# The factor that ScalarE copies out of PSUM: inverse sums in place of the values' products

## The chip, the cores and the metric

The kernel runs on one core of a Trainium2 chip. The metric is the device time of one execution in microseconds (us); less is better. Three runs of the kernel before took 791.66, 791.16 and 791.1 us, so the median is 791.16 us. The engines of the core are named as the profile names them: PE is TensorE's matmul, PEld its weight load, DVE VectorE, ACT ScalarE, POOL GpSimd, SP the queue that issues all DMAs.

## The reference

Eight batches of block-causal attention with eight heads each feed a gated feed-forward block. The two parts in short:

```python
scores = scale * np.matmul(q, k.transpose(0, 1, 3, 2))     # q, k, v: 8 x 8 x 576 x 64
scores = np.where(block_i >= block_j, scores, -1e9)        # blocks of 64 positions
attn = np.exp(scores - np.max(scores, axis=-1, keepdims=True))
attn = attn / (np.sum(attn, axis=-1, keepdims=True) + 1e-09)
out = np.matmul(attn, v)                                   # -> x: 8 x 576 x 512
...
h = gelu(x @ w_in)                                         # 512 -> 1024
u, v = h[..., :512], h[..., 512:]
v_n = (v - mu) / np.sqrt(var + 1e-06) * g_ln
gated = u * (np.einsum('ts,bsd->btd', w_sg, v_n) + b_sg[None, :, None])
y = x + gated @ w_out
```

The change touches only the division by the sums: the kernel multiplies the values' products by the inverse sums, after the product with `v`.

## The kernel before

**Pairs and slots.** The 64 heads are worked in 32 pairs of two; a pair has one *slot* (`slot`, L743), and four slots make a batch. Slot n turns (transposes) the probabilities of pair n and multiplies them with the values, while the scores of pair n+1 are computed in steps in between. Into the slot up to seven *holes* are put (`hole`), each one accumulation of the feed-forward block of an earlier batch. Slots 0 to 3 have no such work to put in: the feed-forward block of batch 0 is queued only when slot 3 is written.

**Order.** PE's order is the order of the code (its instructions are pinned, `kept`); that of ACT, DVE, POOL and SP is made by a scheduler that knows the dependencies. So an edit of the program's code moves other instructions on these engines.

**PSUM.** There are eight banks of 512 numbers per partition. Five (`sbank`) hold score products (tiles `s`), the values' products `ob` and the accumulations of the holes (`accv`, `accu`, `accs`, `acco`). Three (`pbank`) hold transposed data: `pa`, `pb`, `pc` (transposed probabilities, two tiles each per slot), `pd` (of `turn_first`) and `pe` (the transposed inverse sums). With three banks and eight such tiles a slot, the first turns of a slot wait for the last tiles of the slot before to be read out.

**What a slot does, in order.** `inverse` (L443): DVE adds and inverts the row sums (`ri`), POOL spreads them over 64 columns for each head (`rx`). `turn0` writes `pa` twice; ACT copies one into SBUF (`pt`), DVE the other. `turn2` does the same with `pb`. Then come the scores of the next pair: PE writes products into `s`, DVE takes the masked maxima (operation CUSTOM_DVE, `prob<-s`) and ACT the exponents. `av0` starts the values' products in `ob`, `turn1` writes `pc`, two further score steps follow, `turn_first` writes the first 64 positions' probabilities to `pd`. `turn_sums` (L461) transposes the inverse sums of the first 64 positions into columns 128 to 255 of `pd` and those of the other 512 into `pe`. `av1` ends `ob` and `av00` (L488) writes the product of the first 64 positions into columns 256 to 319 of `pd`.

**The end of the slot.** `normalise` (L492) takes a page `x` of 576 columns (one of three buffers shared with the reloaded pages `xr`), lets ACT copy `ob` and the first positions' product into it, lets DVE multiply it in place by `pe` and by the part of `pd`, and issues the store `spill<-x`. `split` (L502) then makes `xh` on DVE (a cast) and, from it, the low parts on POOL; the feed-forward block of that batch multiplies these. `split_qk` prepares the pair after the next: a cast `qk_h` on DVE and two subtractions `qk_l` on POOL.

**Names of the steps.** Below, "pa1" is the second `pa` of a slot, "pb" its first `pb` turn, "the boundary 1 to 2" the stretch in which slot 1 ends and slot 2 begins.

Of the kernel before, what the change touches and what calls it, by code (L numbers as in the profile page):

```python
# [9 lines left out]
F32 = mybir.dt.float32  # L10
# [4 lines left out]
ALU = mybir.AluOpType  # L15
# [13 lines left out]
def kernel(  # L29
# [13 lines left out]
    B, H, D, S = qT.shape  # L43
    P = 128
    BLK = 64
# [23 lines left out]
    def page(dtype, n, name):  # L69
        tag, bufs = KINDS.get(name, KINDS["w"])  # L70
        return sp.tile([P, n], dtype, tag=tag, name=name, bufs=bufs)

    def bank(tag, name, bufs):
        return psum.tile([P, 512], F32, tag=tag, name=name, bufs=bufs)

    def sbank(name):
        return bank("s", name, 5)

    def pbank(name):
        return bank("p", name, 3)  # L80
# [3 lines left out]
    def pin(ins, e):  # L84
        return tc.keep_in_program_order(ins) if e in kept else ins
# [4 lines left out]
    def turn(out, in_, identity):  # L90
        return pin(nc.tensor.transpose(out, in_, identity), "P")  # L91
# [11 lines left out]
    V, A, G, SP = Pinned(nc.vector, "V"), Pinned(nc.scalar, "A"), Pinned(nc.gpsimd, "G"), Pinned(nc.sync, "S")  # L103

    def copy(e, dst, src):
        return {"v": V.tensor_copy, "a": A.copy, "g": G.tensor_copy}[e](dst, src)
# [46 lines left out]
    t = sbank("warm")  # L153
# [15 lines left out]
    for s in (0, 1):  # L169
        t = cp.tile([P, NT, 2 * D], F32, name=f"v_f{s}")  # L170
# [5 lines left out]
    for s in range(4):  # L176
        row = []
        for i in range(NT):
            t = cp.tile([P, P * (i + 1) if i else BLK], F32, name=f"prob{s}_{i}")
# [209 lines left out]
    class Values:  # L389
# [71 lines left out]
        def turn_sums(self):  # L461

            turn(self.t4[:, 128:256], self.rx[:, 0, :], ident)
            t = self.rp = pbank("pe")
            for i in range(1, NT):
                turn(t[:, (i - 1) * P : i * P], self.rx[:, i, :], ident)

        def av(self, dst, j, pts, c0, n, start, stop):
            for a in (0, 1):
                r = slice(a * D, (a + 1) * D)  # L470
                mm(dst[r, :], self.v[:, j, r], pts[a][:, c0 : c0 + n], start=start, stop=stop)
# [19 lines left out]

        def normalise(self):  # L492

            x = self.x = page(F32, S, "x")
            copy("a", x[:, BLK:], self.ob)
            copy("a", x[:, :BLK], self.o0)
            V.tensor_tensor(x[:, BLK:], self.rp, x[:, BLK:], op=ALU.mult)
            V.tensor_tensor(x[:, :BLK], self.t4[:, 128:192], x[:, :BLK], op=ALU.mult)
            spill[self.b, self.p] = dp.tile([P, S], F32, tag="spill", name="spill", bufs=12)
            SP.dma_start(spill[self.b, self.p], x)  # L500

# [380 lines left out]
```

## Time and profile before

| | before |
|---|---|
| median of three runs | 791.16 us |
| the profiled execution | 792.08 us |
| its span, first to last instruction | 790.2 us |
| mean granted TensorE clock | 0.978 |
| ACT COPY x<-ob, 128x512, 32 times | 586 ns each |
| ACT COPY x<-pd, 128x64, 32 times | 217 ns each |
| DVE TENSOR_TENSOR x<-pe, 128x512, 32 times | 686 ns each |
| DVE TENSOR_TENSOR x<-pd, 128x64, 32 times | 213 ns each |

All four operations read PSUM and write the page x. A row of the timeline gives the start, the duration, the engine, the line, the operation with its tiles (written, then read), and in brackets the time that the engine sat idle before it and what ended that. A helper records every operation, so most rows have L88, L91 or L101; the tiles tell which step it is.

### The profile page before, as it was taken

To read this page: it belongs to the slowest core of one execution; us is meant where nothing else is said; L and a number is where in the kernel's file an instruction comes from. 1 tells how busy PE (TensorE), PEld (TensorE's weight loads), DVE (VectorE), ACT (ScalarE), POOL (GpSimd) and SP (SyncE) were. 2 spreads that over 40 slices of the span, in tenths; PEclk is the share of its full clock that TensorE was granted. 3 is DMA by queue.
4 is the path that set the end of the run, shared out by engine and by line. 5 is a ranking of instruction groups with operands and counts; after the bars stand their busy time and mean duration, and the time that the engine had idled before them with its cause. 6 is when DMAs were issued, how large, how long until landed. Compare 5 with 4: busy or idle time off the path is not lost. (4 is left out here: it accounts for less than half of the span.)

```text
span 790.2 us, 15821 instructions
## 1 busy us (share of the span) xinstructions
PE 761.1 (96%) x5926; PEld 639.9 (81%) x5926; DVE 499.7 (63%) x1457; ACT 450.0 (57%) x1172; POOL 267.9 (34%) x331
## 2 busy tenths in 40 slices
PE   7777998999999999999999999999999999999998
PEld 5554786877888888887888888888888978888998
DVE  5897578885757466563866648565676647633532
ACT  4775689567844478435974368544793358721600
POOL 4354255552424113351133414231233510322121
PEclk9897799999999999999999999999999999999999
DMA  7143224212241024311042122410233101320042
GB/s 239 61 126 118 89 91 141 88 61 75 78 149 60 2 76 122 106 61 52 25 136 90 61 76 62 145 50 32 77 106 121 61 19 59 105 76 31 1 121 75
DMA packets 46911, 65.66 MB, mean 83 GB/s; under 512 B 4082, under 2 KB 22514, under 8 KB 46836
## 3 DMA queue, kind: packets, MB, share of 16 engines
q1 hardware_dynamic: 46836, 64.67, 25.6%
q8 instruction: 46, 0.75, 0.4%
q14 instruction: 29, 0.24, 0.1%
HBM read 45.78 MB, written 18.87 MB: 82 GB/s over the span
## 5 line engine op out<-in xcount | busy, mean ns | idle before, releaser
L101 ACT ACTIVATE prob<-prob,negm 128x448 f32<-128x448 f32 (+4 forms) x320 | 176.4, 554 | 40.6 <-DVE negm L101 37.1
L101 POOL TENSOR_TENSOR qk_l<-qk_f,qk_h 128x576 fp32r<-128x576 f32 x62 | 90.9, 1486 | 229.7 <-PE pe L91 92.2
L101 DVE CUSTOM_DVE_ANT_0 prob<-s,mask 128x288 f32<-128x288 f32 (+2 forms) x320 | 117.1, 421 | 56.3 <-PE s L88 56.1
L88 PE MATMUL ob<-pt,v_f 128*64 128x512 f32 (+4 forms) x640 | 107.1, 448 | 0.0
L88 PE MATMUL s<-qk_h 64*128 64x288 f32 (+1 forms) x372 | 88.4, 341 | 3.9 <-ACT u L101 3.7
L101 POOL TENSOR_TENSOR gl<-u,gh 128x288 fp32r<-128x288 f32 x64 | 51.9, 812 | 113.4 <-DVE gh L101 80.2
L88 PE MATMUL s<-qk_l,qk_h 64*128 64x288 f32 (+1 forms) x372 | 83.0, 303 | 0.0
L88 PE MATMUL accu<-xh,wi_h 128*128 128x288 f32 x256 | 78.1, 305 | 0.0
L88 PE MATMUL accs<-ws_h,vh 128*128 128x288 f32 x256 | 78.1, 305 | 0.0
L88 PE MATMUL s<-qk_h,qk_l 64*128 64x288 f32 (+1 forms) x372 | 78.0, 300 | 0.0
L88 PE MATMUL acco<-gh,wo_h 128*128 128x288 f32 x256 | 77.6, 303 | 0.0
L88 PE MATMUL accu<-xl,wi_h 128*128 128x288 f32 x256 | 75.7, 296 | 0.0
L88 PE MATMUL accu<-xh,wi_l 128*128 128x288 f32 x256 | 75.5, 295 | 0.0
L88 PE MATMUL accs<-ws_l,vh 128*128 128x288 f32 x256 | 75.5, 295 | 0.0
L88 PE MATMUL accs<-ws_h,vl 128*128 128x288 f32 x256 | 75.5, 295 | 0.0
L88 PE MATMUL acco<-gh,wo_l 128*128 128x288 f32 x256 | 75.4, 294 | 0.0
L88 PE MATMUL acco<-gl,wo_h 128*128 128x288 f32 x256 | 75.3, 294 | 0.0
L88 PEld LDWEIGHTS ob<-pt,v_f 128*64 128x64 f32 x640 | 37.8, 137 | 41.2 <-issue 32.2
L88 PE MATMUL accv<-wi_h,xh 128*128 128x512 f32 x160 | 66.0, 412 | 3.3 <-POOL xh L101 3.3
L88 PEld LDWEIGHTS s<-qk_h 64*128 64x128 f32 x372 | 63.7, 188 | 5.9 <-ACT u L101 4.9
L88 PEld LDWEIGHTS s<-qk_h,qk_l 64*128 64x128 f32 x372 | 63.8, 187 | 0.0
L88 PE MATMUL accv<-wi_l,xh 128*128 128x512 f32 x160 | 63.8, 399 | 0.0
(104 smaller groups left out, 1924.2 us busy)
## 6 DMA issues: line engine op xcount, KB each, us to landing
spill<-x SPq DMA_DIRECT2D x32, 288.0 KB, 3.7
xr<-spill SPq DMA_DIRECT2D x32, 288.0 KB, 3.2
out_T<-xr SPq DMA_DIRECT2D x32, 288.0 KB, 3.0
qk_f<-in_qT SPq DMA_DIRECT2D x31, 288.0 KB, 3.4
qk_f<-in_kT SPq DMA_DIRECT2D x31, 288.0 KB, 3.8
v_f<-in_v SPq DMA_DIRECT2D x32, 256.0 KB, 3.1
raw<-in_w_in SPq DMA_DIRECT2D x16, 256.0 KB, 4.7
raw<-in_w_out SPq DMA_DIRECT2D x8, 256.0 KB, 5.2
```

The lines of the kernel that those rows point to most:

```text
L88: return pin(nc.tensor.matmul(*a, **k), "P")
L101: return lambda *a, **k: pin(f(*a, **k), self.letter)
```

## The change

`turn_sums` now takes the page x itself, right after the turns, and ACT copies the transposed inverse sums into it: `pe` into the columns from 64 on and the 64 columns of `pd` into the first ones. `normalise` only multiplies: DVE reads `ob` and the product in `pd` from PSUM and multiplies x in place. The number, engines and shapes of the four operations stay.

```diff
         def turn_sums(self):

             turn(self.t4[:, 128:256], self.rx[:, 0, :], ident)
-            t = self.rp = pbank("pe")
+            t = pbank("pe")
             for i in range(1, NT):
                 turn(t[:, (i - 1) * P : i * P], self.rx[:, i, :], ident)
+
+            x = self.x = page(F32, S, "x")
+            copy("a", x[:, BLK:], t)
+            copy("a", x[:, :BLK], self.t4[:, 128:192])
...
         def normalise(self):

-            x = self.x = page(F32, S, "x")
-            copy("a", x[:, BLK:], self.ob)
-            copy("a", x[:, :BLK], self.o0)
-            V.tensor_tensor(x[:, BLK:], self.rp, x[:, BLK:], op=ALU.mult)
-            V.tensor_tensor(x[:, :BLK], self.t4[:, 128:192], x[:, :BLK], op=ALU.mult)
+            x = self.x
+            V.tensor_tensor(x[:, BLK:], self.ob, x[:, BLK:], op=ALU.mult)
+            V.tensor_tensor(x[:, :BLK], self.o0, x[:, :BLK], op=ALU.mult)
             spill[self.b, self.p] = dp.tile([P, S], F32, tag="spill", name="spill", bufs=12)
```

What the scheduler makes of it is shown at the boundary 1 to 2. First ACT, from the last exponents of slot 1 to the first copies of slot 2; before:

```order
L101 ACTIVATE prob_2_112,sums<-prob_2_112,negm 128x320
L101 ACTIVATE prob_2_121,sums<-prob_2_121,negm 128x320
L101 ACTIVATE w<-raw 128x256
L101 COPY x<-ob 128x512
L101 COPY x<-pd 128x64
L101 COPY pt<-pa 128x512
```

and now:

```order
L101 ACTIVATE prob_2_112,sums<-prob_2_112,negm 128x320
L101 COPY x<-pd 128x64
L101 ACTIVATE prob_2_121,sums<-prob_2_121,negm 128x320
L101 ACTIVATE w<-raw 128x256
L101 COPY x<-pe 128x512
L101 COPY pt<-pa 128x512
```

The small copy has moved ahead of the last exponent, and the large one stands where the copy of `ob` stood. Next DVE at the same boundary, from the cast for the pair after the next to the first maximum of the next scores; before:

```order
L101 CAST qk_h<-qk_f 128x1152
L101 TENSOR_SCALAR w<-raw 128x256
L101 SCALAR_TENSOR_TENSOR w<-raw,w 128x256
L101 TENSOR_TENSOR ri<-sums,tiny 128x10
L101 RECIPROCAL ri<-ri 128x10
L101 SCALAR_TENSOR_TENSOR w<-w 128x256
L101 TENSOR_TENSOR x<-pe,x 128x512
L101 TENSOR_TENSOR x<-pd,x 128x64
L101 CAST xh<-x 128x576
L101 COPY pt<-pa 128x512
L101 COPY pt<-pb 128x512
L101 ISA prob_4_134,negm<-s,mask 128x288
```

and now:

```order
L101 CAST qk_h<-qk_f 128x1152
L101 TENSOR_SCALAR w<-raw 128x256
L101 SCALAR_TENSOR_TENSOR w<-raw,w 128x256
L101 TENSOR_TENSOR x<-pd,x 128x64
L101 TENSOR_TENSOR ri<-sums,tiny 128x10
L101 RECIPROCAL ri<-ri 128x10
L101 SCALAR_TENSOR_TENSOR w<-w 128x256
L101 COPY pt<-pa 128x512
L101 TENSOR_TENSOR x<-ob,x 128x512
L101 COPY pt<-pb 128x512
L101 CAST xh<-x 128x576
L101 ISA prob_4_134,negm<-s,mask 128x288
```

The small multiplication has moved ahead of the sums' inverse, and the copies of `pa` and `pb` ahead of the large multiplication and of the cast. Last PE, whose order is the same but whose waits are not; at this boundary, from the last products of slot 1 (`pd<-pt` is av00) to the first `pb` turns, before:

```order
L88 MATMUL pd<-pt_107,v_f_103 64x64 x2
L91 MATMUL pa<-ident,prob_4_134 128x128 [waits PE_49]
L91 MATMUL pa<-ident,prob_3_132 128x128 [waits Activation_49]
L91 MATMUL pa<-ident,prob_2_130 128x128 [waits Activation_49]
L91 MATMUL pa<-ident,prob_1_128 128x128
L91 MATMUL pa<-ident,prob_4_143 128x128 [waits Activation_49]
L91 MATMUL pa<-ident,prob_3_141 128x128
L91 MATMUL pa<-ident,prob_2_139 128x128
L91 MATMUL pa<-ident,prob_1_137 128x128
L91 MATMUL pb<-ident,prob_4_134 128x128 [waits DVE_49]
```

and now:

```order
L88 MATMUL pd<-pt_107,v_f_103 64x64 [waits Activation_49]
L88 MATMUL pd<-pt_107,v_f_103 64x64
L91 MATMUL pa<-ident,prob_4_134 128x128 [waits PE_49]
L91 MATMUL pa<-ident,prob_3_132 128x128
L91 MATMUL pa<-ident,prob_2_130 128x128
L91 MATMUL pa<-ident,prob_1_128 128x128
L91 MATMUL pa<-ident,prob_4_143 128x128 [waits DVE_49]
L91 MATMUL pa<-ident,prob_3_141 128x128
L91 MATMUL pa<-ident,prob_2_139 128x128 [waits Activation_49]
L91 MATMUL pa<-ident,prob_1_137 128x128
L91 MATMUL pb<-ident,prob_4_134 128x128 [waits Activation_49]
```

av00, which writes into `pd`, now waits for ACT to have read the same bank; pa1 waits for DVE (the bank of `pd`, free after the small multiplication) and `pb` for ACT. The wait of av00 on ACT is there in all 32 slots.

## The prediction

> **What bounds the kernel.** I read the page first, then PE's waits, then the timeline at the boundaries.
>
> ```profile
> span 790.2 us, 15821 instructions
> ...
> PE 761.1 (96%) x5926; PEld 639.9 (81%) x5926; DVE 499.7 (63%) x1457; ACT 450.0 (57%) x1172; POOL 267.9 (34%) x331
> ```
>
> PE is busy for 96% of the span, so only two things can shorten the kernel: less time that PE stands idle, or a higher clock while it works. PE's waits, split at 110 us (engine, tile written, what it waited for; us, times, longest), show where it stands idle. First up to 110 us, then behind it:
>
> ```profile
> PE pa L91 <- ACT pt L101: 6.1, 4, 1.9
> PE pb L91 <- DVE x L101: 3.7, 3, 1.4
> PE accv L88 <- POOL xh L101: 3.3, 1, 3.3
> PE pa L91 <- ACT prob L101: 3.1, 3, 1.5
> ```
>
> ```profile
> PE s L88 <- ACT u L101: 3.7, 7, 1.0
> PE pb L91 <- DVE pt L101: 2.1, 1, 2.1
> ```
>
> The waits of `pa`, `pb` and the first `accv` come to 16.2 us in slots 0 to 3, where no hole fills them. In the 680 us behind, the two largest sums make 5.8 us, none of it on x. So the change can gain little after slot 4, where its extra wait (av00 on ACT) must stay covered; slots 0 to 3 decide.
>
> The timeline at the boundary 1 to 2 (start, us, engine, operation, idle before):
>
> ```profile
> 41.45 2.95 POOL L101 TENSOR_TENSOR qk_l<-qk_f,qk_h 128x576 fp32r<-128x576 f32 x2 [1.57 <-PE pe L91]
> ...
> 41.47 0.29 PE L88 MATMUL pd<-pt,v_f 128*64 128x64 f32 x4
> ...
> 41.56 0.55 ACT L101 ACTIVATE prob<-prob,negm 128x320 f32<-128x320 f32 x1
> ...
> 42.90 0.20 ACT L101 COPY x<-pd 128x64 f32<-128x64 f32 x1
> 43.01 0.58 ACT L101 COPY pt<-pa 128x512 f32<-128x512 f32 x1
> 43.07 1.36 DVE L101 TENSOR_TENSOR ri<-sums,tiny 128x10 f32<-128x10 f32 x1
> ...
> 43.64 0.66 PE L91 MATMUL pa<-ident,prob 128*128 128x128 f32 x4 [1.30 <-ACT pt L101]
> ...
> 44.87 0.68 DVE L101 TENSOR_TENSOR x<-pe,x 128x512 f32<-128x512 f32 x1
> ...
> 45.47 0.21 DVE L101 TENSOR_TENSOR x<-pd,x 128x64 f32<-128x64 f32 x1
> ...
> 45.61 1.08 PE L91 MATMUL pb<-ident,prob 128*128 128x128 f32 x7 [1.31 <-DVE x L101]
> ...
> 45.72 0.83 DVE L101 CAST xh<-x 128x576 fp32r<-128x576 f32 x1
> ...
> 48.19 0.46 DVE L101 CUSTOM_DVE_ANT_0 prob<-s,mask 128x288 f32<-128x288 f32 x1 [0.44 <-PE s L88]
> ```
>
> `pb` starts at 45.61, right behind the multiplication that reads `pe` (44.87 + 0.68 = 45.55). That multiplication stood behind `ri`, whose row of 1.36 us ends when POOL's `qk_l` does (41.45 + 2.95 = 44.40). Behind it DVE has still the small multiplication, the cast and the copies, then idles 0.44 us for `s` at 48.19. So DVE and PE alternate: PE waits for DVE's x, then DVE for PE's scores. Only what shortens both is a gain.
>
> **The change part by part.** *The work itself.* These groups carry it (busy us, mean ns, then idle before):
>
> ```profile
> L101 ACT COPY x<-ob 128x512 f32<-128x512 f32 x32 | 18.8, 586 | 20.7 <-POOL qk_l L101 12.4 <-issue 4.9 <-PE ob L88 3.4
> ...
> L101 DVE TENSOR_TENSOR x<-pe,x 128x512 f32<-128x512 f32 x32 | 22.0, 686 | 19.2 <-ACT x L101 19.2
> ...
> L101 DVE CAST xh<-x 128x576 fp32r<-128x576 f32 x32 | 18.7, 602 | 0.6
> ```
>
> Both engines keep a PSUM operation of the same shape: 586 and 686 ns for the large ones, 0.20 and 0.21 for the small ones. No row shows a copy of `pe` on ACT or a product that reads `ob` on DVE; the nearest rows have the same shapes, so busy time changes by nothing.
>
> *The bank of `pe`.* ACT's large copy now frees it. ACT has the small copy (0.20) and the exponent ahead and still starts it at about 42.65, ending near 43.2; before, the bank came free at 45.55.
>
> *The bank of `pd`.* The small multiplication now stands ahead of `ri`, so it runs at 43.07 to 43.28, while `ri` would be held by POOL until 44.40 anyway. `pa1` can follow at 43.3 in place of 43.64, takes its 0.66 us, and `pb` follows at 43.95 in place of 45.61: PE leads by **1.65 us**.
>
> *What av00 pays.* It must now wait for ACT's small copy: behind the exponent that ends at 41.56, that copy ends near 41.8, so av00 slips from 41.47 by 0.35 us. `pa1`'s old wait of 1.30 us covers it. Without that cover it would cost 0.35 us a slot.
>
> *DVE's path.* With PE 1.65 us ahead, DVE's idle time on `pb` and `s` goes. The small multiplication leaves the stretch behind `ri`: 45.47 to 45.72, 0.25 us. The cast took 0.83 us directly behind the multiplication, and 0.60 as the mean of 32; now a copy stands between. The saving lies between 0 and 0.39 us (I estimate the upper end from a cast of 0.44 quoted below); I take 0.2, the distance to the mean. DVE's idle at the boundaries 0 to 1 and 2 to 3, and in the middle of slots 1 and 3:
>
> ```profile
> 32.26 0.69 DVE L101 COPY pt<-pb 128x512 f32<-128x512 f32 x1 [0.65 <-PE pb L91]
> ...
> 33.47 0.46 DVE L101 CUSTOM_DVE_ANT_0 prob<-s,mask 128x288 f32<-128x288 f32 x1 [0.52 <-PE s L88]
> ...
> 38.37 0.62 DVE L101 CUSTOM_DVE_ANT_0 prob<-s,mask 128x448 f32<-128x448 f32 x1 [0.62 <-PE s L88]
> ...
> 61.87 0.69 DVE L101 COPY pt<-pb 128x512 f32<-128x512 f32 x1 [0.37 <-PE pb L91]
> ...
> 63.08 0.46 DVE L101 CUSTOM_DVE_ANT_0 prob<-s,mask 128x288 f32<-128x288 f32 x1 [0.52 <-PE s L88]
> ...
> 66.94 0.62 DVE L101 CUSTOM_DVE_ANT_0 prob<-s,mask 128x448 f32<-128x448 f32 x1 [1.59 <-PE s L88]
> ```
>
> Boundary 0 to 1: 0.65 + 0.52 + 0.25 + 0.2 = 1.62. Boundary 1 to 2: 0.44 + 0.25 + 0.2 = 0.89. Boundary 2 to 3: 0.37 + 0.52 + 0.25 + 0.2 = 1.34. All lie below the lead of 1.65, so DVE sets them. What DVE does not use of PE's lead shortens its next wait: at 66.94 (1.59 us) 1.65 - 1.34 = 0.3, between 0.3 and 1.59; at 38.37 (0.62 us) I take 0.3 too, between 0 and 0.62.
>
> *The boundary 3 to 4.* Here PE waits for the first feed-forward work:
>
> ```profile
> 76.09 2.41 POOL L101 TENSOR_TENSOR wi_l<-w,wi_h 128x256 fp32r<-128x256 f32 x3
> ...
> 76.79 0.44 DVE L101 CAST xh<-x 128x576 fp32r<-128x576 f32 x1
> ...
> 78.46 0.32 POOL L101 TENSOR_TENSOR xh<-x,xh 128x64 fp32r<-128x64 f32 x1
> ...
> 78.83 0.80 PE L88 MATMUL accv<-wi_h,xh 128*128 128x512 f32 x1 [3.26 <-POOL xh L101]
> ```
>
> `accv` waits 3.26 us for POOL's `xh`, which stands behind three `wi_l` (2.41 us, about 0.8 each). Now one of the three comes behind `xh`, which could give up to 1.0 with the small multiplication's 0.25; but the cast now stands behind one copy more (0.68) less that 0.25, so it could lose 0.4. I take 0.5, nearer to the row of POOL, which ends last.
>
> *What is hidden.* The page x is taken some 1.3 us earlier in the slot; its earlier users (stores, reloads) landed long before, except in rival D. The store `spill<-x` is issued by SP behind the next `qk_f` load; the loads that it is moved past go earlier, and nobody reads the spilled page in that slot. The last parts `xl` come about a microsecond later; they multiply only in a later batch's holes. In slots 4 and later PE has holes to do where it waited here, so there I take nothing, between -0.35 (av00, each) and nothing; the smallest margin is rival D's.
>
> **Sum.** 1.62 + 0.89 + 1.34 + 0.3 + 0.3 + 0.5 = 4.95 us. The low end, with no cast saving (-0.6), nothing at 38.37 (-0.3) and the loss at `accv` (-0.9), is 3.15; the high end adds 0.57, 0.32, 1.29 and 0.5, which is 7.63. The profiled execution took 792.08 us (span 790.2), 0.92 above the median 791.16. So 792.08 - 4.95 = 787.13 profiled, **786.2** against the median; own range 783.5 to 788.0.
>
> **The rivals.** A, *the clock is granted again*. Windows around two waits (PEclk is the figure before DMA share and GB/s):
>
> ```profile
> 27.00:30.00 3.00, 0.66 (x4) 0.42 (x4) 2.97 (x6) 1.72 (x5) 2.66 (x5) 0.93 0.33 99
> 30.00:33.50 3.50, 3.43 (x25) 3.10 (x27) 2.30 (x6) 0.59 (x1) 2.38 (x4) 0.50 0.75 247
> ...
> 79.00:87.00 8.00, 8.00 (x39) 5.48 (x40) 4.28 (x16) 4.09 (x12) 1.14 (x1) 0.50 0.53 183
> ```
>
> PE was busy 0.66 of 3 us before 30.00 and then ran at half clock; the 8 us from 79 on, all busy, ran at 0.50 too. If the shorter waits keep the clock up there, 8 us of work take 4, and the sum is 4.95 + 4.0: 782.2. Against it: a wait of over 2.5 us before `accv` stays by my sum. At 0.12. The Trainium skill ("TensorE: Matmul & The Clock Gate", "What's actually happening") has the clock halved after an idle window of about 3.4 us; by it, a wait of 2.76 us in place of 3.26 could miss the window. The trace fits it only loosely: at 30.00 the clock is 0.50 although PE did 0.66 us of work within the 3 us before.
>
> B, *DVE stays the bound*. PE's lead is real, but DVE's chain (`ri` held by POOL to 44.40, then copies, product, cast) ends as late as before, because the copies and the large product now queue for each other; the wait only moves from `pb` to `s`. Then only 0.25 at three boundaries is saved: 0.75, that is 790.4. For it: DVE has next to no idle between 43.07 and 45.72. Against it: the rows of 0.65, 0.52, 0.44, 0.37 and 0.52 us are idle time of DVE itself. At 0.14.
>
> C, *half of it*: DVE's idle goes, but the casts and the middles give nothing and `accv` loses: 1.6 to 3.1 us, 788.0 to 789.6. At 0.13.
>
> D, *av00 turns into a wait*, slower. In every fourth slot the last exponents come late. For slot 9:
>
> ```profile
> 207.08 0.56 ACT L101 ACTIVATE prob<-prob,negm 128x320 f32<-128x320 f32 x1
> ...
> 208.40 0.29 PE L88 MATMUL pd<-pt,v_f 128*64 128x64 f32 x4
> ```
>
> ```profile
> out_T<-xr SPq DMA_DIRECT2D x32, 288.0 KB, 3.0
> ```
>
> ACT's small copy can start when the exponent ends at 207.64 and ends near 207.85; av00 ran at 208.40. Margin 0.55 us. If the page x is still being stored (`out_T<-xr` takes 3.0 us from issue to landing) when ACT wants it, av00 waits up to 3.0 - 0.55 = 2.45 us; in six such slots 14.7, less 4.95 of gain: 800.9. It decides once ACT's copy is more than 0.55 us late. Against it: the previous user of the page is three takings back. At 0.08.
>
> **Chances.** Forecast 0.53, C 0.13, A 0.12, B 0.14, D 0.08. What a measurement can tell from no change is about 0.2%, or 1.6 us; forecast, A and C are faster by more (0.78), B lies within (0.14), D is slower (0.08). The range from A's 782.2 to just above B's 790.4 leaves out D; without B it would hold 0.78.
>
> **What would show it.** Right: in PE's waits `pb` on DVE's x is gone and `pd` waits for ACT's x a few tenths; DVE has no idle before the first `prob<-s` of slots 1 to 3; the first `accv`, at 78.83 before, starts near 78.83 - 4.95 = 73.9; from there the two traces run in parallel. Wrong: the clock between the first `accv` and 8 us later is above 0.50 (A); a wait of PE for DVE's `pt` or of `s` as large as the lost one (B); av00 waits of over 0.3 us in slots 5, 9, 13 and so on (D); or the total differs from what the first `accv` gained.

## The result and the profile after

The changed kernel takes 782.38 us (median of four runs, 781.82 to 783.87) against 791.41 us for the kernel before in the same session: a ratio of 0.9889, with a 95% interval of 0.9874 to 0.9903. It is 9.0 us faster, where 786.2 us had been forecast. The time lies outside the forecast's own range (783.5 to 788.0); it lies inside the wider one only because rival A's 782.2 sets that one's lower end.

The page of the changed kernel, span and busy time:

```profile
span 780.6 us, 15816 instructions
...
PE 753.5 (97%) x5926; PEld 634.9 (81%) x5926; DVE 493.4 (63%) x1457; ACT 447.4 (57%) x1172; POOL 269.1 (34%) x331
```

The span is 9.6 us shorter, but PE's idle time fell only from 790.2 - 761.1 = 29.1 us to 780.6 - 753.5 = 27.1 us. So 7.6 of the 9.6 us are *busy* time of PE, with the same 5926 matmuls. The mean granted clock went from 0.978 to 0.993. That is the first sign that this gain is not one of waits alone.

PE's waits up to 110 us (engine, tile and line, what it waited for; us, times, longest):

```profile
PE pd L88 <- ACT x L101: 4.0, 4, 1.1
PE pd L91 <- ACT pt L101: 3.8, 4, 1.0
PE pa L91 <- ACT prob L101: 2.6, 2, 1.5
PE accv L88 <- POOL xh L101: 2.5, 1, 2.5
PE pa L91 <- DVE x L101: 2.2, 3, 1.6
```

As forecast, `pb`'s wait for DVE's x is gone. In its place stand a wait of av00 for ACT's x (the line of `pd` on L88, 4.0 us in four slots) and one of `pa1` for DVE's x; the wait for ACT's `pt`, 6.1 us of `pa` before, now stands mostly at the turns of the sums (`pd` on L91, 3.8 us). The timeline of the changed kernel at the boundary 1 to 2 (start, us, engine, operation, idle before):

```profile
40.22 0.34 PE L88 MATMUL pd<-pt,v_f 128*64 128x64 f32 x4 [1.08 <-ACT x L101]
...
40.95 0.58 ACT L101 COPY x<-pe 128x512 f32<-128x512 f32 x1
41.21 0.21 DVE L101 TENSOR_TENSOR x<-pd,x 128x64 f32<-128x64 f32 x1
41.34 1.24 DVE L101 TENSOR_TENSOR ri<-sums,tiny 128x10 f32<-128x10 f32 x1
41.47 0.66 PE L91 MATMUL pa<-ident,prob 128*128 128x128 f32 x4 [0.33 <-DVE x L101]
41.96 1.02 PE L91 MATMUL pb<-ident,prob 128*128 128x128 f32 x7
...
44.82 0.45 DVE L101 CAST xh<-x 128x576 fp32r<-128x576 f32 x1
45.19 0.45 DVE L101 CUSTOM_DVE_ANT_0 prob<-s,mask 128x288 f32<-128x288 f32 x1
```

The order is the forecast one: ACT frees `pe` early, DVE's small multiplication runs ahead of `ri`, `pb` follows `pa1` at once, and DVE goes from the cast to the first `prob<-s` without waiting. Measured from the `pd` turn of the sums (37.39 here, 39.85 before), `pb` starts after 4.57 us where it started after 5.76: a lead of 1.19 us, where 1.65 had been forecast.

The slots show where the time went. The table gives the time from the first `pd<-ident,rx` turn of one slot to that of the next, from the timelines (in slots 0 to 4 it starts at 23.70, 39.85, 54.10, 68.43 and 95.81 us before, and at 24.50, 37.39, 50.26, 62.83 and 86.80 after).

| | 0 to 1 | 1 to 2 | 2 to 3 | 3 to 4 |
|---|---|---|---|---|
| before, us | 16.15 | 14.25 | 14.33 | 27.38 |
| after, us | 12.89 | 12.87 | 12.57 | 23.97 |
| shorter by | 3.26 | 1.38 | 1.76 | 3.41 |

That is 9.8 us; in slot 0 these turns come 0.8 us later, and from slot 6 on the lead is between 8.9 and 9.6 us. The two largest pieces, 3.26 and 3.41, are those that the forecast had sized worst.

The granted clock in fine steps shows why. In the profiled execution of before it falls to half at 12.5, 29.6, 46.7, 60.3, 74.0 and 132.0 us and comes back at 16.0, 36.4, 50.1, 63.7, 87.6 and 135.4. To within 0.1 us these times lie on one grid of 3.41 us: 12.5 + 5 x 3.41 = 29.6, + 10 x 3.41 = 46.6, + 14 x 3.41 = 60.2, + 18 x 3.41 = 73.9, + 22 x 3.41 = 87.5. In the changed kernel it falls only at 14.2, 72.3 and 123.5, each time for one step. Windows on that grid (placed to within 0.1 us, so that a clock of 0.99 or 0.51 belongs to the edge); the columns are the window, its length, busy us (and operations) of PE, PEld, DVE, ACT and POOL, then the granted clock, DMA share and GB/s. First before:

```profile
26.25:29.66 3.41, 1.09 (x6) 0.62 (x6) 3.38 (x5) 2.28 (x9) 3.07 (x4) 0.99 0.29 87
29.66:33.07 3.41, 3.00 (x22) 2.67 (x23) 2.61 (x5) 0.78 (x2) 2.72 (x4) 0.50 0.79 257
...
70.62:74.03 3.41, 1.46 (x10) 1.11 (x9) 3.41 (x6) 2.18 (x8) 2.41 (x2) 0.99 0.30 89
...
80.85:84.26 3.41, 3.41 (x27) 2.80 (x27) 2.35 (x9) 0.87 (x2) 0.00 (x0) 0.50 0.81 310
```

and after, at the same two boundaries:

```profile
24.44:27.85 3.41, 2.27 (x19) 1.47 (x20) 3.38 (x11) 3.41 (x15) 1.88 (x2) 1.00 0.02 6
27.85:31.26 3.41, 3.08 (x36) 2.65 (x34) 3.38 (x7) 2.22 (x5) 3.07 (x5) 1.00 0.42 97
...
68.80:72.21 3.41, 1.09 (x5) 0.56 (x3) 3.10 (x6) 0.99 (x3) 2.76 (x4) 1.00 0.69 211
72.21:75.62 3.41, 3.27 (x17) 2.64 (x18) 0.80 (x2) 0.85 (x2) 2.14 (x3) 0.51 0.98 324
```

Before, PE was busy 1.09 of 3.41 us at the boundary 0 to 1, and the clock of the next window was 0.50. After, it was busy 2.27 us, and the clock stayed. At the first feed-forward work the clock fell in both (behind windows of 1.46 and 1.09 us busy), but for 13.6 us before and for 3.4 us after.

The forecast's own signs agree with this. The first `accv` after its wait starts at 72.35 and not at 73.9; it gained 6.5 us while the span gained 9.6, so much of the gain came behind it; and the clock in the 8 us behind it was at half up to 75.7 us and then whole, which was rival A's sign. B's sign (a wait for DVE's `pt` or for `s` as large as the lost one, with only 0.75 us gained) and D's (av00 waiting behind slot 4) are absent.

### The profile page after: what moved, and what is told of

It reads as the page before. It is cut to its first block, busy times and chain, and to the rows that moved or that the text cites. A ratio compares the mean times of both kernels' runs of the same rounds, so it can differ in the third digit from the quotient of the medians.

```text
span 780.6 us, 15816 instructions
## 1 busy us (share of the span) xinstructions
PE 753.5 (97%) x5926; PEld 634.9 (81%) x5926; DVE 493.4 (63%) x1457; ACT 447.4 (57%) x1172; POOL 269.1 (34%) x331
## 5 line engine op out<-in xcount | busy, mean ns | idle before, releaser
L88 PE MATMUL ob<-pt,v_f 128*64 128x512 f32 (+4 forms) x640 | 104.9, 440 | 0.4 <-ACT pt L101 0.2
L88 PE MATMUL s<-qk_h 64*128 64x288 f32 (+1 forms) x372 | 85.9, 332 | 3.7 <-ACT u L101 3.7
L88 PE MATMUL s<-qk_l,qk_h 64*128 64x288 f32 (+1 forms) x372 | 79.7, 296 | 0.0
L88 PE MATMUL accu<-xh,wi_h 128*128 128x288 f32 x256 | 78.2, 305 | 0.0
L88 PE MATMUL accs<-ws_h,vh 128*128 128x288 f32 x256 | 78.1, 305 | 0.0
L88 PE MATMUL acco<-gh,wo_h 128*128 128x288 f32 x256 | 77.5, 303 | 0.0
L88 PE MATMUL accu<-xl,wi_h 128*128 128x288 f32 x256 | 75.6, 295 | 0.0
L88 PE MATMUL accs<-ws_l,vh 128*128 128x288 f32 x256 | 75.5, 295 | 0.0
L88 PE MATMUL accs<-ws_h,vl 128*128 128x288 f32 x256 | 75.4, 295 | 0.0
L88 PE MATMUL acco<-gh,wo_l 128*128 128x288 f32 x256 | 75.4, 294 | 0.0
L88 PE MATMUL acco<-gl,wo_h 128*128 128x288 f32 x256 | 75.3, 294 | 0.0
L88 PE MATMUL accu<-xh,wi_l 128*128 128x288 f32 x256 | 75.3, 294 | 0.0
L88 PE MATMUL s<-qk_h,qk_l 64*128 64x288 f32 (+1 forms) x372 | 74.1, 291 | 0.0
L88 PEld LDWEIGHTS ob<-pt,v_f 128*64 128x64 f32 x640 | 37.5, 136 | 41.5 <-issue 31.9
L88 PE MATMUL accv<-wi_h,xh 128*128 128x512 f32 x160 | 65.3, 408 | 2.5 <-POOL xh L101 2.5
L101 ACT COPY pt<-pa 128x512 f32<-128x512 f32 x32 | 18.6, 580 | 84.3 <-PE pa L91 84.3
L101 DVE TENSOR_TENSOR xr<-acco,xr 128x288 f32<-128x288 f32 x64 | 29.2, 457 | 58.9 <-PE acco L88 48.7
L88 PEld LDWEIGHTS s<-qk_h 64*128 64x128 f32 x372 | 61.5, 180 | 6.1 <-ACT u L101 5.1
```

The source lines that it names most:

```text
L88: return pin(nc.tensor.matmul(*a, **k), "P")
L101: return lambda *a, **k: pin(f(*a, **k), self.letter)
```

## The experiments

**The two theories.** *Clock*: the change shortens PE's idle time at the boundaries, so the clock stays up, and a good part of the gain is PE working at full speed. *Bank*: the gain is the earlier release of `pe` and `pd` and the shorter path on DVE, and the clock only goes along. They come apart when PE's idle time is filled with useless work in the kernel *before*: that gives it the clock and leaves the waits between the other engines as they were, if their order does not change.

**Filling the kernel before (e1) and the changed one (e4).** `pa`'s turns are issued again into the same bank, and the first accumulation of batch 0, whose first six products wait for the last two, does these six again from the start:

```diff
-        def turn0(self, a):
+        def turn0(self, a, n):
             t = pbank("pa")
-            for i in (4, 3, 2, 1):
-                self.turn(a, t[:, (i - 1) * P : i * P], i, 0)
+            for _ in range(1 + FILL.get(n, (0, 0))[a]):
+                for i in (4, 3, 2, 1):
+                    self.turn(a, t[:, (i - 1) * P : i * P], i, 0)
...
+            if b == 0 and st == NT - 1:
+                for _ in range(SIX):
+                    for y, (l, w, c) in enumerate(terms[:6]):
+                        mm(acc, l, w[:, c, DH:], start=(y == 0), stop=(y == 5))
```

In e1 `FILL` is `{1: (1, 3), 2: (1, 3), 3: (1, 3), 4: (2, 0)}` and `SIX` 2; in e4 they are `{4: (2, 1)}` and 1.

> The kernel before, with work added that only fills PE's idle time: pa's turns are issued again into the same bank in slots 1 to 4, and the first six accv products of the first batch are issued two more times. If the clock carries a good part of the gain (theory 'clock'), the granted clock behind the boundaries 0 to 1, 1 to 2 and 2 to 3 (0.50, about 0.6 and 0.57 before) and in the 8 us behind the first late accv (0.50) goes to near 1.0, pb still waits for DVE's x as before (3.7 us, less what the fill takes of it), and the time falls by 3 to 6 us: 785.4 to 788.4. If the earlier release of pe's bank carries all of it (theory 'bank'), the time stays within 0.5 us of 791.4, or rises by what the extra turns delay.

> The changed kernel with such filling in slot 4 only: pa's turns again (two more and one more), the first six accv products once more. In the changed kernel the clock is at half for about 3.4 us from 72.35. Theory 'clock': that stretch goes to full clock, and the time falls by up to 1.7 us, to 780.7 to 781.6. Theory 'bank': no change, 782.4 within 0.5.

e1 took **783.99 us** (783.66 to 784.54), a ratio of 0.9904 (0.9886 to 0.9922) to before: useless work on PE makes the old kernel 8.3 us faster. That is more than I had expected of the clock. A new order on the other engines is not the reason: in the trace of e1 DVE and POOL do the same operations in the same order as before through the whole kernel, and ACT does so up to 82 us, where one copy of `accv` comes ahead of a cast. Windows of e1, whose grid happens to lie as that of before:

```profile
26.25:29.66 3.41, 2.12 (x17) 1.89 (x18) 3.38 (x5) 2.28 (x9) 3.07 (x4) 1.00 0.29 87
29.66:33.07 3.41, 3.41 (x39) 2.73 (x37) 3.38 (x10) 0.95 (x3) 2.79 (x4) 1.00 0.82 250
...
74.03:77.44 3.41, 2.90 (x32) 2.44 (x32) 1.36 (x3) 1.17 (x2) 1.83 (x3) 1.00 0.88 257
77.44:80.85 3.41, 3.41 (x19) 2.31 (x19) 2.83 (x15) 2.60 (x9) 0.00 (x0) 1.00 0.51 200
```

PE is busy 2.12 us where it was 1.09, and the clock stays at 1.00 from 16 us on. e4 took **781.29 us** (780.61 to 781.48; ratio 0.9866, 0.9851 to 0.9881): the falls at 72.3 and 123.5 went, and with them 1.1 us. In the window of the first feed-forward work PE is now busy 2.86 us, and the next one is at full clock:

```profile
68.81:72.22 3.41, 2.86 (x14) 2.02 (x12) 2.49 (x6) 0.97 (x3) 3.18 (x4) 1.00 0.74 213
72.22:75.63 3.41, 2.73 (x30) 2.42 (x30) 1.18 (x2) 1.17 (x2) 2.01 (x3) 1.00 0.88 280
```

"Bank" alone is out, as both of its expectations missed. Slot by slot at full clock:

| | 0 to 1 | 1 to 2 | 2 to 3 | 3 to 4 |
|---|---|---|---|---|
| e1: before, filled, us | 13.50 | 13.51 | 13.35 | 23.38 |
| e4: after, filled, us | 12.89 | 12.87 | 12.57 | 23.04 |
| the change at full clock | 0.61 | 0.64 | 0.78 | 0.34 |
| the clock in the kernel before | 2.65 | 0.74 | 0.98 | 4.00 |

The change by itself is worth 2.37 us in these slots (783.99 - 781.29 = 2.7 in the totals), the clock 8.37. Together that is 10.74 and not the 9.81 of the change, because the changed kernel without filling still loses 23.97 - 23.04 = 0.93 us at 3 to 4. The last column is the weakest: in e4 the scheduler also exchanged some operations of DVE and POOL around the first `accv`. Rows of e1 at the boundary 1 to 2 show what the 0.64 is:

```profile
42.46 0.22 DVE L101 RECIPROCAL ri<-ri 128x10 f32<-128x10 f32 x1
...
43.48 0.21 DVE L101 TENSOR_TENSOR x<-pd,x 128x64 f32<-128x64 f32 x1
43.52 0.74 POOL L101 TENSOR_TENSOR wi_l<-w,wi_h 128x256 fp32r<-128x256 f32 x1
43.72 0.84 DVE L101 CAST xh<-x 128x576 fp32r<-128x576 f32 x1
44.49 0.68 DVE L101 COPY pt<-pa 128x512 f32<-128x512 f32 x1
...
45.69 0.44 DVE L101 CUSTOM_DVE_ANT_0 prob<-s,mask 128x288 f32<-128x288 f32 x1
```

From `ri`'s second step to the first `prob<-s` it is 45.69 - 42.46 = 3.23 us; in the changed kernel (42.61 to 45.19) 2.58. The small multiplication took 0.24 of the difference. The cast took 44.49 - 43.72 = 0.77 to the next start, and takes 45.19 - 44.82 = 0.37 in the changed kernel. In e1 it starts while POOL's `wi_l` runs and ends 0.30 us behind it (43.52 + 0.74 = 44.26); in the changed kernel, where a copy comes between the product and the cast, `wi_l` ends at 44.40, before the cast starts.

**Half of the change (e2, e3).** Only the large operation, and only the small one:

```diff
 e2: turn_sums
-            copy("a", x[:, :BLK], self.t4[:, 128:192])
 e2: normalise
+            copy("a", x[:, :BLK], self.o0)
-            V.tensor_tensor(x[:, :BLK], self.o0, x[:, :BLK], op=ALU.mult)
+            V.tensor_tensor(x[:, :BLK], self.t4[:, 128:192], x[:, :BLK], op=ALU.mult)
...
 e3: turn_sums
-            copy("a", x[:, BLK:], t)
+            self.rp = t
 e3: normalise
+            copy("a", x[:, BLK:], self.ob)
-            V.tensor_tensor(x[:, BLK:], self.ob, x[:, BLK:], op=ALU.mult)
+            V.tensor_tensor(x[:, BLK:], self.rp, x[:, BLK:], op=ALU.mult)
```

> The changed kernel with only the large operation changed: ACT copies pe early and DVE multiplies by ob; for the first 64 positions ACT copies the product and DVE multiplies by pd's inverse sums, as before. av00 then waits for nothing of ACT. Theory 'bank' and theory 'clock' alike: pe's bank is the one that pb waited for, so nearly all of the gain is here, 782 to 785, with the clock up at the three boundaries. Rival 'the small half': pa1 waits for DVE's late small multiplication again, the boundary stays as long, 788 or more.

> The changed kernel with only the small operation changed: pe is read by DVE as before. pb waits for DVE's x again (3 times, some 3 us), the clock falls to half behind the boundaries as before. Both theories: 789 to 792. Rival 'the small half' (the small multiplication off DVE's path, pd's bank free early): 785 or less.

What both theories expected missed, twice. The large half took 789.57 us (786.23 to 791.29 in ten runs; ratio 0.9963, 0.9948 to 0.9978), the small half **785.81** (0.9925, 0.9907 to 0.9943). The rival "the small half" was right for the first and 0.8 us short of right for the second. The profiled execution of e2 is the fastest of its ten, so it shows less trouble than the median has. PE's waits up to 110 us, first of e2, then of e3:

```profile
PE accv L88 <- POOL xh L101: 5.0, 1, 5.0
PE pb L91 <- DVE x L101: 4.6, 3, 1.6
```

```profile
PE pb L91 <- DVE pt L101: 3.5, 3, 1.2
PE pa L91 <- DVE x L101: 3.3, 3, 2.6
```

`pb` takes two banks. With only the large half, its second tile waits for the small multiplication instead, which DVE still does last: the wait for x is 4.6 us, more than the 3.7 of before. I had looked at `pe`'s bank alone. In the four profiles without filling, the clock fell behind the boundaries three times (before), twice (e2: 32.0 and 45.7 us), once (e3: 44.0) and never (after), and in each of them at the first feed-forward work as well.

**The halves, filled (e5, e6).** e2 and e3 with `pb`'s first three turns repeated in slots 1 to 3 (four and three times), and slot 4 filled as in e1 and e4:

```diff
-            for a in (0, 1):
+            for a in (0, *[0] * FILLB.get(n, 0), 1):
                 self.turn(a, t[a][:, 192:320], 4, 2)
```

> The kernel with only the large operation changed, its idle PE time in slots 1 to 4 filled with repeated turns (pb's first three turns four more times in slots 1 to 3, pa's two more in slot 4) and the first six accv products three more times. If its loss against the change (789.6 against 782.4) is the clock, it comes to 781.5 to 784.5 and the clock stays at 1.0 from 20 us on. If it is the bank of pd, which pb's second tile then waits for, it stays at 786 or more.

> The kernel with only the small operation changed, filled in the same way (pb's first turns three more times in slots 1 to 3, pa's two and one more in slot 4, the six accv products once more). Theory 'clock': the two falls of the clock (44.0 and 74.6 in its profile, 3.4 us each at half) go, up to 3.4 us less than 785.8: 782.4 to 784. Theory 'bank': within 0.7 of 785.8.

They took 783.20 us (ratio 0.9889, 0.9876 to 0.9902) and 783.08 (0.9889, 0.9875 to 0.9904), both where theory "clock" had put them. The filling made the large half 6.4 us faster, so its trouble was the clock and not the bank; the small half became 2.7 us faster. With e1 at 0.9904 and e4 at 0.9866, each half holds about half of the change's own worth: the boundaries 0 to 1 and 1 to 2 take 13.20 and 13.21 us in e5, 13.09 and 13.08 in e6, against 13.50 (e1) and 12.88 (e4). The intervals overlap, so this split rests on the slots of one profile each.

**More filling (e7, e8).** Slots 0 and 6 were to be filled too, in the changed kernel and in the one before: in slot 0 nine and thirteen turns of `pa` while its exponents are awaited.

```diff
+                    for _ in range(FILL0[i] if (n, a) == (0, 0) else 1):
                         self.turn(a, t[:, (i - 1) * P : i * P], i, 0)
```

> The changed kernel, filled in slot 4 as before and also in slot 0 (single turns of pa again while the exponents of the first pair are awaited) and in slot 6 (pb's first turns five more times, where pb's second tile waits 2.2 us). Theory 'clock': the fall at 14.2 us goes too, half of 3.4 us less at most: 779.5 to 781.3. Otherwise 781.3 within 0.5.

> The kernel before, filled in slots 0 to 4 and 6: full clock throughout. Theory 'clock': 782 to 783.8, which leaves 2 to 3.5 us between the two kernels at full clock as what the change itself is worth. If the change is worth its 9 us by the order of the work alone, this one stays above 788.

e7 took 785.40 us (ratio 0.9917, 0.9904 to 0.9929) and missed; e8 took 789.55 (0.9975, 0.9958 to 0.9991), where "the order of the work alone" had put it, but for another reason. It stands in PE's waits of e7, and as the same line in e8's:

```profile
PE pb L91 <- ACT pt L101: 4.6, 1, 4.6
```

The extra turns made the scheduler put ACT's instructions in slot 0 in another order; `pb` then waits 4.6 us for ACT's copy, and the clock falls behind that wait. In the profiles the turns of the sums in slot 0 come 4.3 us later than in e4 and 5.5 us later than in e1, about what the totals lose against those two (4.1 and 5.6 us). As tests of the clock in slot 0 they are lost. But e8 gave something else: its twelve runs fall apart by the granted clock. Five with a clock of 0.989 took 791.99 to 792.41 us, the seven with 0.994 to 0.998 took 787.07 to 789.75. The program is the same, and the granted clock goes along with up to 5 us of time.

**Which boundary (e9, e10).** e1's filling in slots 1 to 3 alone (`SIX` 0), and in slot 4 alone.

> The kernel before with the filling only in slots 1 to 3 (pa's turns), none in slot 4. From the slots of the fully filled one (2.65, 0.74 and 0.98 us shorter than before, and 4.00 in slot 3 to 4): 4.4 us faster, 787 to 788, with the clock at half still from about 74 to 87.6. If the parts do not add up (a stretch of full clock early only makes a longer wait at the first late accv), less than 2 us.

> The kernel before with the filling only in slot 4 (pa's turns two more times, the six accv products two more times). By the same table 4.0 us faster, 787 to 788.3, with the clock at half behind the boundaries 0 to 1, 1 to 2 and 2 to 3 as before, and at 1.0 from 74 us on. If the 8 us at half clock were hidden behind another engine: within 1 us of 791.8.

e9 took 786.27 us against 791.78 (ratio 0.9933, 0.9910 to 0.9957), 5.5 us faster; e10 787.88 (0.9955, 0.9936 to 0.9973), 3.9 us. They add up to 9.4 against e1's 8.3, within what their intervals allow. In e10 the clock falls at 28.4, 45.5 and 59.2 us as before, and its slots take 15.92, 14.20, 14.33 and 23.39 us: only the last is e1's. In e9 they take 13.50, 13.49, 13.35 and 24.81. Its last one is 2.57 us shorter than before though nothing was filled in it: the late fall lasts 3.4 us (76.0 to 79.4) and not the 13.6 that I expected. The order of the work on DVE, ACT and POOL is that of before through the whole kernel, and the first late `accv` waits no shorter:

```profile
75.28 0.50 PE L88 MATMUL accv<-wi_h,xh 128*128 128x512 f32 x1 [3.44 <-POOL xh L101]
```

So the boundaries also decide how the next waits lie on the grid, and that place, not the length of the wait, made most of the 13.6 us.

**The roles swapped, nothing early (e11).** Both copies of the inverse sums stand in `normalise` again:

```diff
 turn_sums
-            x = self.x = page(F32, S, "x")
-            copy("a", x[:, BLK:], t)
-            copy("a", x[:, :BLK], self.t4[:, 128:192])
+            self.rp = t
 normalise
-            x = self.x
+            x = self.x = page(F32, S, "x")
+            copy("a", x[:, BLK:], self.rp)
+            copy("a", x[:, :BLK], self.t4[:, 128:192])
```

> The changed kernel with the two copies of the inverse sums put back to the place where the products were copied (in normalise, behind av00): roles swapped, but nothing issued early. By the order of its instructions the small multiplication stands behind the large one again, so pb waits for DVE as in the kernel before. If the early place is what matters: 788 to 791, with falls of the clock at some boundaries. If the swap alone is enough (ACT, not DVE, frees pe): 782 to 784.

It took 789.68 us (ratio 0.9973, 0.9961 to 0.9986), with the clock at half from 30.0 to 36.8, 47.0 to 50.4, 60.7 to 64.1 and 77.8 to 84.6 us, and slots of 16.01, 14.07, 14.18 and 26.19 us. That is where the expectation had put it if the early place matters. So the swap alone is worth 2.1 us (0.9961 to 0.9986 is 1.1 to 3.1); the rest hangs on the copies being issued early, which lets the small multiplication run ahead of `ri`. e2, where the large copy stands early and the small operation is as before, took the same (789.57): the early place of the large copy alone brought no more than the swap.

e4 is the fastest of all: its four runs (780.61 to 781.48 us) lie below the four of the changed kernel (781.82 to 783.87), though they come from two sessions and the intervals of the two ratios overlap.

## Why the prediction came out as it did

**Right: the order and its first effect.** `pb`'s wait for DVE's x went, the small multiplication moved ahead of `ri` at no cost, and `pb` started right behind `pa1` (41.96 and 41.47 us). That no busy time is added holds: ACT's copy of `pe` takes 573 ns where that of `ob` took 586, DVE's multiplication by `ob` 671 where that by `pe` took 686, and the totals of both engines fell (499.7 to 493.4 and 450.0 to 447.4 us). Behind slot 5 the lead stays between 8.9 and 9.6 us, so the new wait of av00 stayed covered there, and D did not happen.

**Too small: DVE's path.** I took 0.25 for the small multiplication and 0.2 for the cast, with 0.39 as the upper end. At full clock the boundaries show 0.61, 0.64 and 0.78 us: 0.24 and 0.40. The upper end was the true one, but the neighbour that counts is not the copy in between, it is POOL. In the kernel before, 15 of the 32 casts took 0.60 to 0.90 us; each of these started while an operation of POOL was running and ended 0.31 or 0.32 us behind the end of that. The other 17 took 0.44 to 0.46, 16 of them with POOL idle at their start, and two of those directly behind the multiplication. At the boundary 1 to 2 it is `wi_l`, which ends at 46.24 in the kernel before, after the cast's start at 45.72. The copy in between only puts the cast behind it. The mean of 0.60, to which I took the distance, mixed the two kinds.

**Wrongly explained: DVE's idle time.** I put 0.65 + 0.52, 0.44, 0.37 + 0.52, 0.3 and 0.3 us, 3.1 of my 4.95, down to PE's lead of 1.65 us. In e1 the bank of `pe` is freed as late behind `ri` as before (from RECIPROCAL's start 42.46 to 43.55, against 44.46 to 45.55), and the slots are still 2.65, 0.74 and 0.98 us shorter. The five idle rows at the boundaries are gone in e1, and so is the one at 38.37: DVE had waited because PE made the scores at half clock or came late from it. Only in the middle of slot 3 is PE's lead needed too: the row of 1.59 us is 1.18 in e1 and 0.18 in the changed kernel. So the amount came about, but mostly by the clock, and larger: 3.26, 1.38 and 1.76 us against 1.92, 0.89 and 1.64.

**Missed: the clock at 3 to 4.** The largest miss is one term: 0.5 us forecast, 3.41 measured, of which 0.34 is the change at full clock. Rival A named it, with the right price (8 us at half clock are 4 us of work; e10 measures 3.9), and had 0.12. My reason against it was that a wait of over 2.5 us would stay before `accv`. It did stay, 2.5 us, and the clock did fall. But it fell for one step of the grid and not for four. I had weighed only whether it falls, not how long it stays down. The rows of the two kernels, before and after:

```profile
72.86 0.66 PE L91 MATMUL pa<-ident,prob 128*128 128x128 f32 x4 [1.95 <-ACT pt L101]
...
78.83 0.80 PE L88 MATMUL accv<-wi_h,xh 128*128 128x512 f32 x1 [3.26 <-POOL xh L101]
```

```profile
67.84 0.66 PE L91 MATMUL pa<-ident,prob 128*128 128x128 f32 x4 [1.57 <-DVE x L101]
...
72.35 0.80 PE L88 MATMUL accv<-wi_h,xh 128*128 128x512 f32 x1 [2.46 <-POOL xh L101]
```

Before, the clock had already fallen at 74.0, behind the window with `pa1`'s wait of 1.95 us; the wait of `accv`, from 75.57 to 78.83, then took parts of two windows and kept it down. After, the window with `pa1`'s wait left the clock up, and the wait of `accv`, from 69.89 to 72.35, lay in one window. e9 shows that this is a matter of place: there the two waits are longer, 2.13 and 3.44 us, and the clock is down for one step too.

**A's number is partly luck.** A's 782.2 adds 4.0 us behind `accv` to the forecast's waits. What was measured is 2.9 us more than the forecast at 3 to 4, 2.0 us more in the three slots before it, mostly by the clock there, which A shows at the boundary 0 to 1 but does not price, and 0.8 us less in slot 0. That these come to A's sum within 0.2 us is luck.

**av00 cost more than 0.35 us.** In slots 0 to 3 it waits up to 1.1 us for ACT's small copy, since the exponent ahead of that copy now ends 2.58 us behind the `pd` turn of the sums (39.97 against 37.39) where it was 1.71 before (41.56 against 39.85). I had carried the old distance over. In e1 that distance is 2.59 us (39.83 against 37.24), so it comes with the earlier PE and not with the change. Little came of it: `pa1` behind it waits for DVE in any case.

What stays open: how much of the clock's share the changed kernel would keep with another position of the grid. Its four runs differ by 2 us, and the start of the grid differs from execution to execution (12.5, 14.2, 11.6 and 13.2 us for the first fall of before, after, e2 and e3). Whether PE's lead alone, at half clock, would have ended DVE's waits was not tried.

## What to carry to other kernels

Before a stall of the matrix engine is priced, look at the granted clock in the windows *behind* it: here stalls of 1 to 3 us pulled the clock down, and full clock alone, with the waits of the other engines in place, was worth 8.3 us. Filling the idle time with repeated, harmless work is the test that parts the two. It is a clean one only where the other engines keep their order, as in e1 and e9 and not in e7 and e8. And a bank's release has to be followed for every tile that takes a bank, since freeing the one that was waited for lets the next one be the last.

## What the runs showed of the hardware

The clock changes only at times on a grid of 3.41 us, whose position against the start of the kernel differs between executions. The Trainium skill ("TensorE: Matmul & The Clock Gate", "What's actually happening") states a free-running window of 4096 cycles, 3413 ns: the traces agree. It also says that the clock halves after a window that is idle. The runs show that less is enough. Four windows of e3, where the first and the last are followed by half clock and the other two are not (the next windows start at 43.92, 57.57, 71.22 and 74.63):

```profile
40.50:43.92 3.42, 1.94 (x14) 1.15 (x11) 3.38 (x7) 1.61 (x4) 3.08 (x5) 1.00 0.43 107
...
54.16:57.57 3.41, 1.80 (x13) 1.28 (x14) 3.30 (x6) 1.81 (x6) 3.41 (x5) 1.00 0.55 172
...
67.81:71.22 3.41, 1.45 (x9) 1.27 (x10) 3.41 (x12) 1.60 (x5) 1.08 (x3) 1.00 0.69 213
71.22:74.63 3.41, 0.92 (x4) 0.46 (x3) 2.14 (x4) 0.35 (x2) 3.41 (x6) 1.00 0.51 153
```

The window with 1.94 us of work lost the clock, those with 1.80 and 1.45 kept it. In the thirteen profiles of this case, on each one's grid, the clock fell behind every full-clock window in which PE was busy less than 1.43 us and behind none with more than 2.06 (e8, from 136.00); between these both happened. So no single threshold in busy time as the profile draws it parts the two.

The way back up can take more than one busy window. In before the windows from 74.03 and 77.44 were busy 1.54 and 2.02 us and each was followed by another at half; so was the one from 80.85, which was busy throughout, and only behind the next busy one was the clock whole again. Behind the boundaries 1 to 2 and 2 to 3 of before, and in the changed kernel (72.21, busy 3.27 us), one window was enough. So the same kind of stall, a wait of PE of 2 to 3 us for `xh`, went with 13.6 us of half clock in the one kernel and with 3.4 in the other.

The casts `xh` show a DVE operation held by POOL. In before and in the changed kernel each one that started well inside a running operation of POOL ended 0.31 to 0.36 us behind it and took up to 0.98 us; with POOL idle it took 0.44 to 0.46, whatever stood before it on DVE.
